# Attention scores by quarters of the array, and h by column halves, in a kernel of chunk attention and two experts

## The chip, the cores and the metric

One core of one Trainium2 chip. The time is that of the device for one execution, in microseconds; the kernel before took 1265.45 us (median of 3 runs).

## The reference

Three stages follow each other; all of them are in float32. B, H, S, D are 8, 8, 576, 64.

```python
q_c, k_c, v_c = (a.reshape(B, H, S // 64, 64, D) for a in (q, k, v))
scores = D ** -0.5 * q_c @ k_c.transpose(0, 1, 2, 4, 3)
attn = np.exp(scores - scores.max(-1, keepdims=True))
attn = attn / (attn.sum(-1, keepdims=True) + 1e-09)
x = (attn @ v_c).reshape(B, H, S, D).transpose(0, 2, 1, 3).reshape(4608, 512)

h = x @ w_in                                  # 512 -> 1024
e = np.exp(h - h.max(-1, keepdims=True))
u = h * (e / (e.sum(-1, keepdims=True) + 1e-09))
mu = u.mean(-1, keepdims=True); var = ((u - mu) ** 2).mean(-1, keepdims=True)
y = ((u - mu) / np.sqrt(var + 1e-06) * g_ln) @ w_out

h2 = y @ w_in2                                # 512 -> 2048
out = np.maximum(0.01 * h2, h2) @ w_out2
```

The weights arrive as 64-bit floats; the kernel converts them itself.

## The kernel before

There are 36 tiles of 128 tokens (`T = 36`). A tile holds two chunks of 64 tokens (index c in the code) for eight heads; two heads (index e) lie one above the other on the 128 partitions, and four such pairs (`KD = 4`) side by side. The order of all instructions is written out by hand (`manual_schedule`): every engine gets its own instructions in the order in which the program calls them.

The first part, up to about 556 us, is one loop over t. In the iteration of t the kernel works on several tiles at once: the scores of tile t + 3 (t + 2 in the first five iterations, `AHEAD = 5`), the softmax of the same, the probabilities' transposition and the product with v for tile t + 1, the first product h of tile t, the activation SoLU and the sums of the layer norm of tile t - 1, the transposition of the normalised tile t - 2, and one group of 24 matmuls of the second product y. Beside that it converts the weights of all products from 64-bit words, in pieces (one or two in an iteration, `DOUBLE`), on ScalarE, VectorE and GpSimd. The second part, the second expert, runs from there to the end; it takes its data through DRAM.

What an iteration calls, in the order of the program, for t > 5 and not "late":

- `solu_a(t-1)`: VectorE's maximum over the 1024 columns of h (L438), ScalarE's exponential with its sum (L440)
- `ff1_mm(t, 0)`: the first 12 matmuls of h of tile t (L423)
- `solu_b(t-1)`: VectorE's product of h and exponential with its sum (L445)
- `pt_mm(t+1)` (L379), `softmax_b(t+2)`: VectorE's sum and reciprocal (L366 to L368), GpSimd's multiplication of es (L369)
- `convert_a`, `convert_b`: VectorE's conversions (L108 to L118); for the pieces of w_out GpSimd's scaling by g (L171)
- `pt_copy(t+1)`: ScalarE's copy of the probabilities (L385)
- `solu_c(t-1)`: GpSimd's small columns (L451, L454, L455), ScalarE's square with its sum (L457), which has the product's sum as its bias; `solu_d(t-1)`: GpSimd normalises (L463 to L467)
- `y1_group`: 24 matmuls of y (L505), ScalarE's copy of y (L513)
- `attend(t)`: x of tile t + 1 (L395), scores of tile t + 3 (L346), the split of x into a high part (ScalarE, L409) and a low part (VectorE, L413), the start of softmax (VectorE L357, L359; ScalarE L362)
- `lnT_mm(t-2)`: eight transposes in two halves (L478), `lnT_split`: high part on ScalarE (L489), low part on VectorE (L493)
- `ff1_mm(t, 1)`: the other 12 matmuls of h

Every fourth iteration (t = 5, 9, 13, ... 33) is "late": the transposes and the split stand ahead of x there, and the group of y stands at the end. In the iterations up to t = 5 the group of y is missing, the conversions stand at the end, and x of the next tile comes after the second half of h. In the code's first stretch (before the loop) `exponentials`, `maxima`, `factors` and `probabilities` do the softmax of tiles 0 to 2.

PSUM has eight banks. Before: two for `ef` (in turn for lnT's halves and for y), four for h (two tiles of two banks), one `ptx` for the probabilities and x, one `s` for the scores. Since `ef` has two banks, the first half of lnT waits for an earlier user, and the second half for the copy of the y of the same iteration.

The scores of a pair of heads come from one matmul for each chunk: q of both heads is stationary (128 rows, 64 columns), and the moving operand is a tile `kbd` in which the keys of the two heads stand on the diagonal, with zeros beside them, so that 128 columns come out.

Of the kernel before, what the change touches and what calls it, by code (L numbers as in the profile page):

```python
# [17 lines left out]
P = 128  # L18
# [3 lines left out]
FF1 = 1024  # L22
# [30 lines left out]
def kernel(  # L53
# [252 lines left out]
    with tc.manual_schedule():  # L306

        with ExitStack() as phase:
# [4 lines left out]
                tc.tile_pool(name="psh", bufs=2, space=bass.MemoryType.PSUM)  # L313
# [4 lines left out]
            kbd = [pa.tile([P, 2, KD, 2, D], F32, tag=f"kbd{i}", bufs=1, name=f"kbd{i}") for i in range(2)]  # L318
# [4 lines left out]
            def load_qk(t, eng=sync):  # L323
# [4 lines left out]
                kb = kbd[t % 2]  # L328
                for e in range(2):
                    eng.dma_start(out=kb[e * D : (e + 1) * D, e], in_=k[t, e * D : (e + 1) * D])  # L330
# [10 lines left out]
            def qk_mm(t):  # L341
                ps = s_ps[t] = bank("ef" if t in (1, 2) else "s", "s_ps").rearrange("p (h n) -> p h n", h=H)
                kb, qq = kbd[t % 2], qt.pop(t)
                for i in range(KD):
                    for c in range(2):
                        pe.matmul(  # L346
                            ps[c * D : (c + 1) * D, 2 * i : 2 * i + 2, :],
                            lhsT=qq[:, i, c * D : (c + 1) * D],
                            rhs=kb[:, :, i, c, :],
                            start=True,  # L350
                            stop=True,
                        )

            def softmax_a(t):
                ps = s_ps.pop(t)
                sm = st8[t] = pa.tile([P, 2, H], F32, tag="st8", name="st8")
                dve.reduce_max(sm[:, 0, :], ps, axis=AX)  # L357
                e = es[t] = pa.tile([P, H, D], F32, tag="es", name="es")
                dve.tensor_tensor(  # L359
                    e, ps, sm[:, 0, :].unsqueeze(2).to_broadcast([P, H, D]), op=ALU.subtract  # L360
                )
# [53 lines left out]
            def ff1_mm(t, half):  # L415
                if half == 0:
                    hs[t] = psh.tile([P, 2, 512], F32, tag="h", name="h_ps")
                x, h = xs[t], hs[t]
                for kk in (0, 1) if half == 0 else (2, 3):
                    w = slots["wi1", kk // 2].rearrange("p e (a n f) -> p e a n f", a=2, n=2)  # L420
                    for a, b in ((0, 0), (0, 1), (1, 0)):
                        for n in range(2):
                            pe.matmul(  # L423
                                h[:, n, :],
# [9 lines left out]

            def solu_a(t):
                h = hs[t].rearrange("p n f -> p (n f)")
                z = sol[t] = wk.tile([P, 8], F32, tag="z", bufs=3, name="z")
                dve.reduce_max(z[:, 0:1], h, axis=AX, negate=True)  # L438
# [164 lines left out]
            def warm(n):  # L603
                for _ in range(n):
                    pe.transpose(spare[:, 0, :P], ident, ident)
# [485 lines left out]
```

## Time and profile before

| what | value |
|---|---|
| median of 3 runs | 1265.45 us (1265.34 to 1266.11) |
| profiled execution, its own time | 1266.24 us |
| span of its instructions | 1264.5 us |
| PE, busy | 1237.8 us, 98% of the span, 7978 instructions |
| DVE, busy | 874.0 us, 69% |
| ACT, busy | 566.5 us, 45% |
| POOL, busy | 269.7 us, 21% |
| mean granted TensorE clock | 0.997 |

PE is TensorE's matmuls, PEld its weight loads, DVE is VectorE, ACT ScalarE, POOL GpSimd. A float32 matmul of the program appears as two instructions of PE. Shares over the span mix the first part with the second, so they say little of an engine's load in one iteration.

### The profile page before, as it was taken

The numbers are of one execution on the slowest core, as the hardware profiler recorded it, in microseconds if no ns is written. First come the engines' busy times: TensorE is split into PE (matmuls) and PEld (weight loads), VectorE is DVE, ScalarE is ACT, GpSimd is POOL, SyncE is SP. The second block draws the span as 40 slices with busy tenths as digits, with TensorE's granted clock in tenths as the row PEclk, the third lists the DMA queues.
The fourth block names the chain that finished last, engine by engine and source line by source line (L and its number), as shares of the span: only waits on it lengthen the run. The fifth ranks groups of instructions, "written<-read, shape, count | busy, mean of one in ns | idle before, by whom it ended". The sixth has DMA issues, their size and how long they took to land.

```text
span 1264.5 us, 21471 instructions
## 1 busy us (share of the span) xinstructions
PE 1237.8 (98%) x7978; PEld 1100.1 (87%) x7978; DVE 874.0 (69%) x1356; ACT 566.5 (45%) x1006; POOL 269.7 (21%) x356
## 2 busy tenths in 40 slices
PE   5999999999999999999999999999999999999998
PEld 4778888878888887899989988998999899989987
DVE  8677767867786777435686677577657766775675
ACT  6646444545544555334433344344235343442351
POOL 0356545644655565200000000000000000000000
PEclk9999999999999999999999999999999999999999
DMA  9525456755575573549889878987898899789676
GB/s 245 155 79 173 147 162 204 237 185 159 187 227 184 162 233 101 192 137 332 265 293 306 294 240 275 309 272 243 293 310 254 260 296 304 242 260 299 202 217 199
DMA packets 171639, 288.74 MB, mean 228 GB/s; under 512 B 50576, under 2 KB 81296, under 8 KB 170512
## 3 DMA queue, kind: packets, MB, share of 16 engines
q1 hardware_dynamic: 171152, 286.78, 71.7%
q8 instruction: 64, 1.05, 0.3%
q10 hardware_dynamic: 384, 0.59, 0.1%
q14 instruction: 39, 0.32, 0.1%
HBM read 239.08 MB, written 48.23 MB: 227 GB/s over the span
## 4 chain that ended last, share of the span: by engine, by line
PE 88%; DVE 6%; ACT 2%; DMA 2%; issue 1%; POOL 0%; SPq 0%; ACTq 0%
PE h_ps L835 28%; PE o_ps L892 19%; PE y_ps L505 14%; PE h_ps L423 12%; PE o_ps L903 10%; PE x_ps L395 2%; PE s_ps L346 2%; PE ln_ps L478 2%; PE pt_ps L379 1%; DVE lnT L493 1%; DVE wf L114 1%; DMA kbd<-in_k 1%; DMA raw<-in_w_in 1%; DVE us L445 1%; DVE wf L110 1%
## 5 line engine op out<-in xcount | busy, mean ns | idle before, releaser
L835 PE MATMUL h_ps<-yo,w_s 128*128 128x384 f32 x2016 | 351.0, 334 | 0.0
L835 PEld LDWEIGHTS h_ps<-yo,w_s 128*128 128x128 f32 x2016 | 349.3, 188 | 0.7
L892 PE MATMUL o_ps<-wo_s,yo 128*128 128x512 f32 (+1 forms) x1016 | 262.9, 393 | 0.0
L423 PE MATMUL h_ps<-wi,xs 128*128 128x512 f32 x864 | 209.9, 396 | 2.8 <-ACT xs L409 1.6
L505 PE MATMUL y_ps<-lnT,wo 128*128 128x512 f32 (+1 forms) x888 | 205.6, 388 | 2.7 <-DVE lnT L493 1.9
L892 PEld LDWEIGHTS o_ps<-wo_s,yo 128*128 128x128 f32 x1016 | 179.0, 188 | 28.7
L505 PEld LDWEIGHTS y_ps<-lnT,wo 128*128 128x128 f32 x888 | 161.0, 188 | 37.4 <-DVE lnT L493 4.4
L423 PEld LDWEIGHTS h_ps<-wi,xs 128*128 128x128 f32 x864 | 159.1, 188 | 37.9 <-ACT xs L409 2.6
L903 PEld LDWEIGHTS o_ps<-wo_s,yo 128*128 128x128 f32 x1008 | 144.6, 188 | 15.6
L271 DVE TENSOR_TENSOR yo<-c,yo 128x768 fp32r<-128x768 f32 x144 | 132.4, 951 | 32.0 <-ACT yo L270 32.0
L903 PE MATMUL o_ps<-wo_s,yo 128*128 128x256 f32 x1008 | 149.7, 283 | 0.0
L814 ACT ACTIVATE c<-h_c 128x384 f32<-128x384 f32 x144 | 72.9, 526 | 127.3 <-DVE h_c L846 127.3
L846 DVE TENSOR_TENSOR h_u<-h_ps,h_p 128x384 f32<-128x384 f32 x96 | 53.2, 554 | 106.8 <-PE h_ps L835 100.0
L270 ACT ACTIVATE yo<-c 128x768 fp32r<-128x768 f32 x144 | 113.0, 835 | 7.1 <-DVE c L876 5.5
L445 DVE SCALAR_TENSOR_TENSOR us<-h_ps,us 128x1024 f32<-128x1024 f32 x36 | 44.1, 1224 | 50.9 <-ACT us L440 50.9
L369 POOL TENSOR_TENSOR es<-es,st 128x512 f32<-128x512 f32 x33 | 34.6, 1047 | 163.7 <-DVE st L368 163.7
L493 DVE TENSOR_TENSOR lnT<-ln_ps,lnT 128x512 fp32r<-128x512 f32 x72 | 46.1, 682 | 33.4 <-ACT lnT L489 33.3
L270 ACT ACTIVATE yo<-a 128x768 fp32r<-128x768 f32 x36 | 29.8, 837 | 72.5 <-DVE a L265 72.5
L846 DVE TENSOR_TENSOR h_c<-h_ps,h_u 128x384 f32<-128x384 f32 x96 | 53.1, 553 | 12.8 <-PE h_ps L835 12.3
L440 ACT ACTIVATE us<-h_ps,z 128x1024 f32<-128x1024 f32 x36 | 40.1, 1115 | 43.0 <-DVE z L438 42.9
L362 ACT ACTIVATE es<-es 128x512 f32<-128x512 f32 x33 | 20.9, 632 | 82.7 <-DVE es L359 82.4
L814 ACT ACTIVATE c<-h_ps 128x384 f32<-128x384 f32 x48 | 23.6, 492 | 76.2 <-PE h_ps L835 76.2
(91 smaller groups left out, 1412.9 us busy)
## 6 DMA issues: line engine op xcount, KB each, us to landing
w_s<-wi_d SPq DMA_DIRECT2D x336, 256.0 KB, 4.0
wo_s<-wo_d SPq DMA_DIRECT2D x168, 512.0 KB, 4.6
wi_d<-wi SPq DMA_DIRECT2D x8, 1792.0 KB, 6.5
wo_d<-wi SPq DMA_DIRECT2D x8, 1792.0 KB, 6.7
raw<-in_w_out SPq DMA_DIRECT2D x24, 512.0 KB, 4.8
raw<-in_w_in SPq DMA_DIRECT2D x23, 512.0 KB, 5.1
vbd<-in_v SPq DMA_DIRECT2D x72, 128.0 KB, 4.3
a<-y_d SPq DMA_DIRECT2D x24, 384.0 KB, 5.2
```

Source lines behind the costliest of these rows:

```text
L270: act.activation(o[:, 0], x, AF.Copy)
L271: dve.tensor_tensor(o[:, 1], x, o[:, 0].bitcast(F32), op=ALU.subtract)
L423: pe.matmul(h[:, n, :], lhsT=x[:, a, kk, :], rhs=w[:, b, kk % 2, n, :], start=(kk == 0 and a == 0 and b == 0), stop=(kk == KD - 1 and a == 1),
L440: act.activation(u, h, AF.Exp, bias=z[:, 0:1], accum_out=z[:, 1:2])
L445: dve.scalar_tensor_tensor(u, h, 1.0 / FF1, u, op0=ALU.mult, op1=ALU.mult, accum_out=z[:, 2:3])
L493: dve.tensor_tensor(dst[:, 1], ps, dst[:, 0].bitcast(F32), op=ALU.subtract)
L505: pe.matmul(ps[:, part], lhsT=w[:, a, kk % 4, m * P : (m + 1) * P], rhs=lnT[:, c, kk, pairs, :][:, part], start=(kk == 0 and a == 0 and c ...
L814: act.activation(blocks[block, j // 2][:, j % 2], src, AF.Prelu, alpha=0.01)
L835: pe.matmul(ps, lhsT=w[:, a, kk * P : (kk + 1) * P], rhs=y[:, c, kk, :], start=(first and kk == 0 and a == 0 and c == 0), stop=(kk == 1 an ...
L846: dve.tensor_tensor(o, ps, x, op=ALU.add)
L892: pe.matmul(ps[:, : 2 * P * (a.stop - a.start)], lhsT=x[:, 0, kk, m * P : (m + 1) * P], rhs=w[:, kk, a].rearrange("p a n -> p (a n)"), sta ...
L903: pe.matmul(sums[p % 2][m][:, : 2 * P], lhsT=x[:, 1, kk, m * P : (m + 1) * P], rhs=w[:, kk, 0], start=False, stop=(i == PAIRS - 1 and kk = ...
```

## The change

- Scores: the key tile has no zeros any more (`kbs`, one DMA). Each head of a pair has its own matmul on 64 rows and 64 columns of the array, so four quarters are in use, and the results of the heads e = 0 and e = 1 go to two banks, `s0` and `s1`. The maxima and the subtraction of the softmax are made bank by bank.
- h: from t = 2 on, the first call of `ff1_mm` computes columns 0 to 511 over all of the contraction, the second columns 512 to 1023. Each half has a bank of its own out of three. The maximum of the first half is taken in the iteration of the tile itself, that of the second in the next; VectorE takes the minimum of the two negated maxima. Exponential and product run by halves, and GpSimd adds the two halves' sums (`solu_c`) ahead of its other columns and of the square.
- In the late iterations the transposes and the split of the layer norm are called ahead of the conversions.
- Names of banks in the second part follow (`s` becomes `s0` or `s1`; one bank of o is now `s1`).

```diff
             psh = phase.enter_context(
-                tc.tile_pool(name="psh", bufs=2, space=bass.MemoryType.PSUM)
+                tc.tile_pool(name="psh", bufs=3, space=bass.MemoryType.PSUM)
...
-            kbd = [pa.tile([P, 2, KD, 2, D], F32, tag=f"kbd{i}", bufs=1, name=f"kbd{i}") for i in range(2)]
+            kbs = [pa.tile([P, KD, 2, D], F32, tag=f"kb{i}", bufs=1, name=f"kb{i}") for i in range(2)]
...
-                kb = kbd[t % 2]
-                for e in range(2):
-                    eng.dma_start(out=kb[e * D : (e + 1) * D, e], in_=k[t, e * D : (e + 1) * D])
+                eng.dma_start(out=kbs[t % 2], in_=k[t])
...
             def qk_mm(t):
-                ps = s_ps[t] = bank("ef" if t in (1, 2) else "s", "s_ps").rearrange("p (h n) -> p h n", h=H)
-                kb, qq = kbd[t % 2], qt.pop(t)
+                ps = s_ps[t] = [
+                    bank("ef" if t == 1 else f"s{e}", "s_ps").rearrange("p (h n) -> p h n", h=H)[:, :KD]
+                    for e in range(2)
+                ]
+                kb, qq = kbs[t % 2], qt.pop(t)
                 for i in range(KD):
-                    for c in range(2):
-                        pe.matmul(
-                            ps[c * D : (c + 1) * D, 2 * i : 2 * i + 2, :],
-                            lhsT=qq[:, i, c * D : (c + 1) * D],
-                            rhs=kb[:, :, i, c, :],
-                            start=True,
-                            stop=True,
-                        )
+                    for e in range(2):
+                        r = slice(e * D, (e + 1) * D)
+                        for c in range(2):
+                            pe.matmul(
+                                ps[e][c * D : (c + 1) * D, i, :],
+                                lhsT=qq[r, i, c * D : (c + 1) * D],
+                                rhs=kb[r, i, c, :],
+                                start=True,
+                                stop=True,
+                            )
...
-                dve.reduce_max(sm[:, 0, :], ps, axis=AX)
                 e = es[t] = pa.tile([P, H, D], F32, tag="es", name="es")
-                dve.tensor_tensor(
-                    e, ps, sm[:, 0, :].unsqueeze(2).to_broadcast([P, H, D]), op=ALU.subtract
-                )
+                for i in range(2):
+                    dve.reduce_max(sm[:, 0, i::2], ps[i], axis=AX)
+                for i in range(2):
+                    m = sm[:, 0, i::2].unsqueeze(2).to_broadcast([P, KD, D])
+                    dve.tensor_tensor(e[:, i::2], ps[i], m, op=ALU.subtract)
...
-                if half == 0:
-                    hs[t] = psh.tile([P, 2, 512], F32, tag="h", name="h_ps")
-                x, h = xs[t], hs[t]
-                for kk in (0, 1) if half == 0 else (2, 3):
+                if t < 2:
+                    ks, ns = ((0, 1), (2, 3))[half], (0, 1)
+                else:
+                    ks, ns = range(KD), (half,)
+                for n in ns if t >= 2 or half == 0 else ():
+                    if t == 1 and n == 1:
+                        hs[t, n] = bank("ef", "h_ps")
+                    else:
+                        hs[t, n] = psh.tile([P, 512], F32, tag="h", name="h_ps")
+                x = xs[t]
+                for kk in ks:
                     w = slots["wi1", kk // 2].rearrange("p e (a n f) -> p e a n f", a=2, n=2)
                     for a, b in ((0, 0), (0, 1), (1, 0)):
-                        for n in range(2):
+                        for n in ns:
                             pe.matmul(
-                                h[:, n, :],
+                                hs[t, n],
                                 lhsT=x[:, a, kk, :],
                                 rhs=w[:, b, kk % 2, n, :],
...
+            def solu_max(t, n):
+                if n == 0:
+                    sol[t] = wk.tile([P, 12], F32, tag="z", bufs=3, name="z")
+                dve.reduce_max(sol[t][:, 8 + n : 9 + n], hs[t, n], axis=AX, negate=True)
+
             def solu_a(t):
-                h = hs[t].rearrange("p n f -> p (n f)")
-                z = sol[t] = wk.tile([P, 8], F32, tag="z", bufs=3, name="z")
-                dve.reduce_max(z[:, 0:1], h, axis=AX, negate=True)
+                z = sol[t]
+                dve.tensor_tensor(z[:, 0:1], z[:, 8:9], z[:, 9:10], op=ALU.min)
                 u = us[t] = wk.tile([P, FF1], F32, tag="us", bufs=3, name="us")
-                act.activation(u, h, AF.Exp, bias=z[:, 0:1], accum_out=z[:, 1:2])
+                for n in range(2):
+                    c = slice(n * 512, (n + 1) * 512)
+                    act.activation(
+                        u[:, c], hs[t, n], AF.Exp, bias=z[:, 0:1], accum_out=z[:, 8 + n : 9 + n]
+                    )
 
             def solu_b(t):
-                h = hs.pop(t).rearrange("p n f -> p (n f)")
                 z, u = sol[t], us[t]
-                dve.scalar_tensor_tensor(
-                    u, h, 1.0 / FF1, u, op0=ALU.mult, op1=ALU.mult, accum_out=z[:, 2:3]
-                )
+                for n in range(2):
+                    c = slice(n * 512, (n + 1) * 512)
+                    dve.scalar_tensor_tensor(
+                        u[:, c],
+                        hs.pop((t, n)),
+                        1.0 / FF1,
+                        u[:, c],
+                        op0=ALU.mult,
+                        op1=ALU.mult,
+                        accum_out=z[:, 10 + n : 11 + n],
+                    )
...
                 z, u = sol[t], us[t]
+                for n in (1, 2):
+                    a = 6 + 2 * n
+                    pool.tensor_tensor(
+                        z[:, n : n + 1], z[:, a : a + 1], z[:, a + 1 : a + 2], op=ALU.add
+                    )
...
-                eng.memset(kbd[i][0:D, 1], 0.0)
-                eng.memset(kbd[i][D:P, 0], 0.0)
...
+                    if t < 3:
+                        solu_max(t - 1, 0)
+                    solu_max(t - 1, 1)
                     solu_a(t - 1)
...
@@ -737,6 +770,10 @@
                     softmax_b(t + 2)
                 if t <= AHEAD or (late and t < T - 1):
                     pt_copy(t + 1)
+                if late and t >= 2:
+                    lnT_mm(t - 2)
+                    lnT_split(t - 2, 0)
+                    lnT_split(t - 2, 1)
                 if t > AHEAD:
                     if late:
                         take_magnitudes(pieces)
@@ -744,10 +781,8 @@
                     convert_b(pieces)
                 if AHEAD < t < T - 1 and not late:
                     pt_copy(t + 1)
-                if late and t >= 2:
-                    lnT_mm(t - 2)
-                    lnT_split(t - 2, 0)
-                    lnT_split(t - 2, 1)
+                if 1 < t < T:
+                    solu_max(t, 0)
                 if 1 <= t <= T:
                     solu_c(t - 1)
                     solu_d(t - 1)
...
```

## Rows read from the trace of the kernel before

**Rows 1.** Stretches: length, then busy us of PE, PEld, DVE, ACT, POOL; granted clock; DMA.
```profile
66.24:503.29 437.05, 429.80 (x3202) 355.03 (x3201) 326.75 (x520) 224.30 (x394) 246.61 (x306) 1.00 0.57 175
...
109.41:123.81 14.40, 14.40 (x110) 11.94 (x109) 11.16 (x19) 8.42 (x15) 9.39 (x13) 1.00 0.58 163
...
555.76:1264.50 708.74, 705.11 (x4040) 659.94 (x4039) 475.67 (x711) 279.96 (x456) 0.00 (x0) 1.00 0.84 271
```

**Rows 2.** Waits of the whole span: engine, line, releaser: us, times, longest.
```profile
PEld x_ps L395 <- ACT pt L385: 7.6, 10, 2.7
...
PEld y_ps L505 <- DVE lnT L493: 4.4, 8, 1.7
```

**Rows 3.** Timeline of TensorE, t = 6: start us, us, engine, line, operation.
```profile
101.03 1.15 PE L395 MATMUL x_ps<-pt,vbd 128*64 128x64 f32 x32
...
102.01 1.05 PE L346 MATMUL s_ps<-kbd,qt 128*64 128x128 f32 x16
...
102.99 0.86 PEld L478 LDWEIGHTS ln_ps<-ident,us 128*128 128x128 f32 x8 [0.17 <-issue]
```

**Rows 4.** Instruction groups by line and shape, VectorE.
```profile
L438 DVE TENSOR_REDUCE z<-h_ps 128x1 f32<-128x1024 f32 x36 | 43.7, 1214 | 3.7 <-PE h_ps L423 3.7
...
L357 DVE TENSOR_REDUCE st<-s_ps 128x8 f32<-128x512 f32 x33 | 22.3, 677 | 0.0
```

**Rows 5.** Timeline of ScalarE and GpSimd, t = 3.
```profile
60.64 1.15 ACT L457 ACTIVATE sq<-us,z 128x1024 bf16<-128x1024 f32 x1
...
61.78 1.06 ACT L489 ACTIVATE lnT<-ln_ps 128x512 fp32r<-128x512 f32 x2
...
62.74 0.59 ACT L409 ACTIVATE xs<-x_ps 128x512 fp32r<-128x512 f32 x1
...
62.95 0.19 POOL L451 TENSOR_SCALAR z<-z 128x1 f32<-128x1 f32 x1
...
63.22 0.19 POOL L454 TENSOR_TENSOR z<-z 128x1 f32<-128x1 f32 x1
```

**Rows 6.** The same, t = 1 (first two) and t = 2.
```profile
43.22 0.60 ACT L409 ACTIVATE xs<-x_ps 128x512 fp32r<-128x512 f32 x1 [0.48 <-PE x_ps L395]
...
43.83 0.19 POOL L451 TENSOR_SCALAR z<-z 128x1 f32<-128x1 f32 x1
...
50.53 0.19 POOL L451 TENSOR_SCALAR z<-z 128x1 f32<-128x1 f32 x1
...
52.20 0.60 ACT L409 ACTIVATE xs<-x_ps 128x512 fp32r<-128x512 f32 x1 [1.77 <-PE x_ps L395]
```

**Rows 7.** Timeline of GpSimd, t = 6, and in the last row t = 7.
```profile
103.08 2.42 POOL L171 TENSOR_TENSOR wf<-wf,g_sb 128x512 f32<-128x512 f32 x2 [2.84 <-DVE wf L118]
...
105.59 0.19 POOL L451 TENSOR_SCALAR z<-z 128x1 f32<-128x1 f32 x1
...
119.23 0.19 POOL L451 TENSOR_SCALAR z<-z 128x1 f32<-128x1 f32 x1
```

**Rows 8.** Stretches at t = 4, columns as in rows 1.
```profile
70.22:73.00 2.78, 0.48 (x8) 0.22 (x8) 2.75 (x6) 2.53 (x5) 0.02 (x1) 1.00 0.85 280
...
73.00:76.40 3.40, 3.40 (x49) 3.07 (x46) 1.61 (x5) 3.01 (x6) 2.07 (x6) 0.50 0.34 99
```

**Rows 9.** Timeline of GpSimd and VectorE, t = 12 (first two) and t = 16.
```profile
188.07 0.65 POOL L454 TENSOR_TENSOR z<-z 128x1 f32<-128x1 f32 x1
...
189.42 0.69 DVE L413 TENSOR_TENSOR xs<-x_ps,xs 128x512 fp32r<-128x512 f32 x1
...
246.90 0.24 POOL L451 TENSOR_SCALAR z<-z 128x1 f32<-128x1 f32 x1
...
247.23 0.65 POOL L454 TENSOR_TENSOR z<-z 128x1 f32<-128x1 f32 x1
...
248.50 0.68 DVE L413 TENSOR_TENSOR xs<-x_ps,xs 128x512 fp32r<-128x512 f32 x1
```

More of the change, by code (lines that the diff above doesn't have):

```diff
@@ L473, in lnT_mm @@
                 for hf in range(2):
-                    tag = ("s", "ptx")[hf] if t == T - 2 else "ef"
+                    tag = ("s0", "ptx")[hf] if t == T - 2 else "ef"
                     ps = ln_ps[t, hf] = bank(tag, "ln_ps").rearrange("p (i n) -> p i n", i=4)
@@ L496, in y1_group @@
                 pairs = (slice(0, 2), slice(0, 3, 2), slice(1, 3))[b % 3]
-                bnk = bank("s" if (b, m) == (NB - 1, 0) else "ef", "y_ps")
+                bnk = bank("s1" if (b, m) == (NB - 1, 0) else "ef", "y_ps")
                 ps = bnk.rearrange("p (a n) -> p a n", a=2)
@@ L577, in exponentials @@
                         es[t][:, h],
-                        ps[:, h],
+                        ps[h % 2][:, h // 2],
                         AF.Exp,
@@ L587, in maxima @@
                 es[t] = pa.tile([P, H, D], F32, tag="es", name="es")
-                dve.reduce_max(sm[:, 0, :], s_ps[t], axis=AX)
+                for i in range(2):
+                    dve.reduce_max(sm[:, 0, i::2], s_ps[t][i], axis=AX)
                 dve.tensor_scalar_mul(sm[:, 0, :], sm[:, 0, :], -scale)
@@ L599, in probabilities @@
                     act.activation(es[t][:, h], es[t][:, h], AF.Copy, scale=sm[:, 1, h : h + 1])
-            spare = psh.tile([P, 2, 512], F32, tag="h", name="spare")
+            spare = psh.tile([P, 512], F32, tag="h", name="spare")
             def warm(n):
                 for _ in range(n):
-                    pe.transpose(spare[:, 0, :P], ident, ident)
+                    pe.transpose(spare[:, :P], ident, ident)
             qk_mm(0)
@@ L825, in h2_product @@
                 if i == 0:
-                    banks[n, chain] = bank(("ptx", "s")[at], "h2_ps")[:, :TH]
+                    banks[n, chain] = bank(("ptx", "s0")[at], "h2_ps")[:, :TH]
                 else:
@@ L916, in out_banks @@
             if p == 1:
-                sums[1] = [pso.tile([P, 512], F32, tag=f"b{m}", name="o_ps") for m in range(3)]
+                sums[1] = [pso.tile([P, 512], F32, tag=f"b{m}", name="o_ps") for m in range(2)]
+                sums[1].append(bank("s1", "o_ps"))
             else:
@@ L921, in out_banks @@
                 if apart:
-                    sums[0][:2] = [bank(tag, "o_ps") for tag in ("ptx", "s")]
+                    sums[0][:2] = [bank(tag, "o_ps") for tag in ("ptx", "s0")]
                 sums["whole"] = None if apart else o
```

## Prediction

> **What bounds the kernel now.** I read the stretches first. From 66 to 503 us, where attention and the first expert run interleaved, TensorE is busy 429.80 of 437.05 us, and in the second expert behind it 705.11 of 708.74 [rows 1]; there the change only gives other bank names. So work taken off TensorE counts, and so does every hole cut into its queue. Then the waits [rows 2]: what holds TensorE is small, 7.6 us of weight loads behind the probabilities' copy (L385) and 4.4 us behind the split of the layer norm (L493). Last the timeline, tile by tile, for who stands behind whom. Two things matter there. In the first tiles (t = 1 to 5 of the loop) TensorE is not the bound: ScalarE, VectorE and GpSimd pass each tile on, and the next h waits for the split of x. From t = 6 on TensorE has no slack, but it needs ScalarE in every tile: the layer norm's second half takes its bank from the copy of y (L513).
>
> **Scores by quarters.** Today a tile's 16 score instructions of 128 columns take 102.99 - 102.01 = 0.98 us, and the 32 of 64 columns before them 102.01 - 101.03 = 0.98 us [rows 3]: the two column halves already overlap, since 0.98/32 = 0.031 us is about half of what 64 columns cost if 128 cost 0.98/16 = 0.061. After: 32 instructions of 64 columns. If all four quarters run at once, half of 0.98, so 0.49; if only the column halves do, 0.98 as in the row above. The layout now changes between x and the scores too; at the change behind the scores the weight load waits 0.17 us for nothing that the profile shows [rows 3]. So a tile gains 0.49 at best, loses 0.17 at worst. I take four at once and one more change: 0.49 - 0.17 = 0.32, call it 0.3. The row is nearest to that, because the column halves overlap fully.
>
> The Trainium skill has a rule against this edit: in TensorEngine Tiling, Key Properties, a change of tiling mode (not of the tile alone) drains the engine. The 0.17 us of rows 3 agrees that a change costs; by that rule the gain is 0.3 a tile, and by a free change it would be 0.49.
>
> **The loads and the masks.** K comes in one DMA in place of two, and the zeroed key tiles go. Both sit ahead of the first scores or beside a busy TensorE: I count nothing, with half a microsecond either way.
>
> **h by halves, on VectorE.** A maximum over 1024 takes 1.214 us, over 512 0.677 [rows 4], so a split costs 2 x 0.677 - 1.214 = 0.14. There are four such splits (maximum of h, product, maximum of scores, subtraction), and a minimum of one column: below 0.8 us a tile. Against it the first half's exponential lets the product start after half of ScalarE's work, and the first half's maximum moves out of the way. I count the two as equal, bounds -0.5 to +0.5 a tile. Where TensorE leads this is hidden.
>
> **The sums of the halves, on GpSimd.** This is the costly edit. The square (L457, ScalarE) takes the product's sum as its bias. VectorE delivers it with the product today. Afterwards GpSimd adds two columns first, and those adds stand where L451 stands now: behind the multiplication of es (L369), which waits for softmax's reciprocal. At t = 3 the square starts at 60.64, L451 only at 62.95 [rows 5]. L451 with the gap behind it takes 0.27 there and L454, an addition of one column, 0.19; from these I take 0.45 for two adds. So the square starts at 62.95 + 0.45 = 63.40, 2.8 us late, and what is behind it on ScalarE moves too: 63.40 + 1.14 for the square (61.78 - 60.64) + 0.96 for the two lnT copies (62.74 - 61.78) = 65.50 for the copy of x, which started at 62.74. That is +2.8 on the path, since h of the next tile needs x.
>
> - t = 4 has the same pattern: +2.8.
> - t = 1: 43.83 + 0.45 + 1.14 = 45.42 for x, not 43.22: +2.2 [rows 6].
> - t = 2: 50.53 + 0.45 + 1.14 + 0.96 = 53.08, not 52.20: +0.9 [rows 6].
> - t = 5 is late by little; not counted.
>
> First tiles: 2.8 + 2.8 + 2.2 + 0.9 = +8.7 us. The three banks of h also make the second half of h wait for the first half of the tile before (the product at t = 3); but that ends before the late copy of x and is covered by it. If TensorE were at half clock there the cover would fail, which is the upper bound of +13; the lower is 6, with VectorE's gain taken at every tile.
>
> At t = 6 and 7 GpSimd has two scalings of w_out (L171) ahead of L451, which wait for VectorE's conversions. At t = 6 the sum is ready at 105.59 + 0.45 = 106.04, the square ends its turn at 107.18, and the copy of y, as long as that of x (0.60 [rows 6]), ends at 107.78 [rows 7]. TensorE wants that bank for the second half of lnT, four transposes after 102.99, at 103.43. It stands for 4.3 us, and the copy of x behind it is late by as much, so VectorE's conversions and L171 of t = 7 are too. There L451 comes at 119.23 today [rows 7]; 4.3 us later and with the adds, square and copy it is 119.23 + 4.3 + 0.45 + 1.14 + 0.60 = 125.7, where the second half of lnT is due one tile (14.40 us [rows 1]) after 103.43, at 117.8: +7.9. With the two tiles' 0.3 us on TensorE taken off, t = 6 and 7 together: +7.3 (bounds 5.5 and 9).
>
> A stand of that length also lowers the clock: after 70.22 to 73.00, in which TensorE worked 0.48 of 2.78 us, it was granted half, 1.2 GHz, for 3.40 us [rows 8]. One such stretch costs 3.40/2 = 1.7. That behind t = 6 falls into the wait of t = 7; that behind t = 7 counts: +1.7 (0 to 3.4).
>
> **From t = 9 on** the loop repeats every eight tiles, three times. At t = 16 L451 comes at 246.90, and beside VectorE an add costs 0.65 (L454) [rows 9]: sum at 246.90 + 1.2 = 248.1, square to 249.25, copies of y and x start at 249.25 and 249.75, x's low part at 250.4 in place of 248.50, +1.9; VectorE carries it through the next tile's exponential to the probabilities' copy, which TensorE waits for in the late tiles (L385 in rows 2). I take +1.7. At t = 12 L454 runs at 188.07, and by the same steps the low part of x, 189.42 today, comes near 190.5 [rows 9]; an estimate is that half of it is slack, +0.6. The split ahead of the conversions takes away what is left of the wait of L505 in the late tiles, -0.6 (4.4 us over 8 waits [rows 2]), and four of the eight tiles keep their 0.3: -1.2. Sum +0.5 for eight tiles, +1.5 for 24. Bounds -4.5 (0.49 a tile, t = 12 without a wait) to +6 (quarters that don't overlap).
>
> **Sum.** 8.7 + 7.3 + 1.7 + 1.5 = +19.2 us. The profiled execution took 1266.24 us with a span of 1264.5; the median of the runs is 1265.45, 0.8 below it. 1266.24 + 19.2 = 1285.4 for such an execution, and 1284.7 for the median; I say 1285.
>
> **Rivals.**
> - *The square stays hidden, faster.* If the sum reaches ScalarE within the idle time ahead of its next work, all waits fall away; then some 33 tiles give 0.3 us, 9.9, and three late tiles 0.6, 1.8: 1253.7. For it: a busy TensorE covers ScalarE in most tiles. It decides at 1.8 us, the longest such idle time in the first tiles [rows 6]; against it, L451 starts 2.3 us behind the square in rows 5. Chance 0.10.
> - *The quarters don't overlap across the row halves.* The edit then does not do what it says: 0.98 + 0.17 for the scores, 0.48 us worse than counted in the some 16 tiles where TensorE sets the pace: +7.7, 1292.4. For it: the trace shows column halves only. Chance 0.13.
> - *TensorE does not wait at t = 6 and 7*, because the two banks of lnT and y fall otherwise. Then 7.3 + 1.7 go: 1275.7. Against it: the bank order follows the calls, and they don't change. Chance 0.10.
> - *About no change*, the losses of the first tiles being half and the gain 0.49: chance 0.04.
>
> My forecast has 0.63. A difference under 0.2% (2.5 us) can hardly be told from none. Slower: 0.63 + 0.13 + 0.10 = 0.86; faster 0.10; same 0.04. The bounds of the terms add to 6 + 5.5 + 0 - 4.5 = +7 and 13 + 9 + 3.4 + 6 = +31; from 1268 to 1298 all slower cases are in and 0.14 is left out.
>
> **What the profile after would show.** Right: the square waits for GpSimd's column in nearly every tile, 2 to 3 us in the first ones and over 7 at t = 6 and 7; TensorE idles some 4 us ahead of the second half of lnT in both of these; 32 score instructions in about half a microsecond. The second expert takes as long as before. Wrong: the square right behind the product, or TensorE without a hole near 105 us. What would undo the prediction most is a first-tile path that has slack that I took for none.

## The result, and the profile after

The changed kernel takes 1279.53 us (median of 5 runs, 1277.58 to 1280.57) against 1265.45: ratio 1.0109, 95% interval 1.0094 to 1.0123, so it is slower by 14 us. The forecast was 1285 with a range of 1268 to 1298. The profiled execution took 1279.53 us with a span of 1277.7, against 1266.24 and 1264.5: 13.3 us more, and the text below accounts for those.

Stretches of the kernel after, columns as in [rows 1]. The first answers to the first of [rows 1], from the transposes of the probabilities at t = 4 to the same point behind the last tiles; the second is the second expert.

```profile
71.68:516.71 445.03, 426.51 (x3666) 350.79 (x3664) 340.47 (x698) 229.05 (x455) 261.12 (x364) 0.99 0.54 171
568.81:1277.70 708.89, 705.05 (x4040) 659.87 (x4039) 475.91 (x711) 279.96 (x456) 0.00 (x0) 1.00 0.85 271
```

The second expert is as long as before (708.89 and 708.74). In the first stretch TensorE has less work (426.51 us for 429.80) and stands idle for 18.5 us, where it was idle for 7.3. So TensorE was indeed relieved, and holes cost more than that was worth. Waits of the whole span, columns as in [rows 2]:

```profile
ACT sq L488 <- POOL z L479: 80.5, 35, 7.0
...
PE ln_ps L509 <- ACT ys L544: 10.5, 5, 3.9
PE h_ps L434 <- ACT xs L413: 5.5, 5, 2.3
PE h_ps L434 <- DVE us L465: 5.5, 2, 2.9
...
PEld x_ps L399 <- ACT pt L389: 5.2, 12, 0.6
```

The square (L488) waits for GpSimd's added column 35 times in 36. Three waits of TensorE hang on it or on the third bank: the layer norm's second half (L509), h for the copy of x, and h for the product that reads its bank (L465). Against that, the wait for the probabilities' copy is shorter than in [rows 2], and that of y for the layer norm's split (4.4 us there) is gone.

Timeline of ScalarE and GpSimd at t = 3, which answers to [rows 5], and ahead of it ScalarE's copies of x at t = 1 and 2, which answer to [rows 6]:

```profile
44.86 0.58 ACT L413 ACTIVATE xs<-x_ps 128x512 fp32r<-128x512 f32 x1
...
54.79 0.60 ACT L413 ACTIVATE xs<-x_ps 128x512 fp32r<-128x512 f32 x1
...
62.59 0.59 ACT L389 ACTIVATE pt<-pt_ps 128x512 f32<-128x512 f32 x1
64.44 1.04 POOL L373 TENSOR_TENSOR es<-es,st 128x512 f32<-128x512 f32 x1 [3.77 <-DVE st L372]
65.45 0.34 POOL L479 TENSOR_TENSOR z<-z 128x1 f32<-128x1 f32 x2
65.82 1.15 ACT L488 ACTIVATE sq<-us,z 128x1024 bf16<-128x1024 f32 x1 [2.64 <-POOL z L479]
66.97 1.06 ACT L520 ACTIVATE lnT<-ln_ps 128x512 fp32r<-128x512 f32 x2
67.92 0.60 ACT L413 ACTIVATE xs<-x_ps 128x512 fp32r<-128x512 f32 x1
```

The square used to follow the copy of the probabilities at once. Now ScalarE stands for 2.64 us, until GpSimd has multiplied es (L373) and made its two additions (0.34 us, together with the gap behind them 0.4). The copy of x starts 1.6, 2.6 and 5.2 us later than in [rows 5, 6].

GpSimd and ScalarE at t = 6 and 7, which answer to [rows 7], and TensorE at t = 6, which answers to [rows 3]:

```profile
109.04 2.42 POOL L171 TENSOR_TENSOR wf<-wf,g_sb 128x512 f32<-128x512 f32 x2 [2.84 <-DVE wf L118]
111.42 0.33 POOL L479 TENSOR_TENSOR z<-z 128x1 f32<-128x1 f32 x2
...
111.79 1.15 ACT L488 ACTIVATE sq<-us,z 128x1024 bf16<-128x1024 f32 x1 [6.97 <-POOL z L479]
112.94 0.58 ACT L544 ACTIVATE ys<-y_ps 128x512 f32<-128x512 f32 x1
...
130.51 0.33 POOL L479 TENSOR_TENSOR z<-z 128x1 f32<-128x1 f32 x2
```

```profile
107.25 1.15 PE L399 MATMUL x_ps<-pt,vbd 128*64 128x64 f32 x32
108.34 0.69 PE L349 MATMUL s_ps<-kb,qt 64*64 64x64 f32 x32
108.96 0.66 PE L509 MATMUL ln_ps<-ident,us 128*128 128x128 f32 x4
113.57 1.11 PE L509 MATMUL ln_ps<-ident,us 128*128 128x128 f32 x4 [3.95 <-ACT ys L544]
...
132.66 1.11 PE L509 MATMUL ln_ps<-ident,us 128*128 128x128 f32 x4 [2.20 <-ACT ys L544]
```

This is the chain of the forecast, link by link: scalings, additions, square, copy of y, and TensorE's second four transposes 3.95 us late at t = 6 and 2.20 us at t = 7. The scores now take 108.96 - 108.34 = 0.62 us instead of 0.98, and the product with V before them 1.09 instead of 0.98.

Stretches at the stand of t = 6, behind it and behind that of t = 7, and then two at t = 4, which answer to [rows 8]:

```profile
109.70:113.57 3.87, 0.00 (x1) 0.01 (x1) 0.47 (x1) 1.78 (x4) 2.94 (x9) 0.82 0.80 261
112.20:119.00 6.80, 5.43 (x15) 4.47 (x16) 3.30 (x7) 4.44 (x9) 3.08 (x6) 0.50 0.73 228
132.70:136.10 3.40, 3.40 (x10) 2.85 (x11) 2.02 (x5) 1.32 (x3) 1.71 (x2) 0.50 0.80 258
70.30:76.05 5.75, 2.85 (x20) 2.31 (x18) 5.61 (x14) 1.96 (x6) 1.47 (x2) 1.00 0.28 86
76.05:79.45 3.40, 3.40 (x26) 2.63 (x28) 2.10 (x6) 0.76 (x3) 1.53 (x4) 1.00 0.48 167
```

TensorE was granted half (1.2 GHz) for 6.8 us behind t = 6 and for 3.4 us behind t = 7. In early_from_8 (below), whose program is the same up to t = 7, it was 3.4 us behind t = 6 and none behind t = 7, so these lengths differ from run to run. At t = 4, where [rows 8] show 0.50, the clock stays full: there it had worked 2.85 us of the 5.75 before, in place of 0.48 of 2.78.

Instruction groups of VectorE and GpSimd by shape, which answer to [rows 4]:

```profile
L449 DVE TENSOR_REDUCE z<-h_ps 128x1 f32<-128x512 f32 x72 | 48.8, 680 | 4.0 <-PE h_ps L434 3.9
...
L479 POOL TENSOR_TENSOR z<-z 128x1 f32<-128x1 f32 x72 | 18.1, 272 | 10.7 <-ACT us L457 9.6 <-DVE us L465 1.1
```

A maximum over half a row takes 680 ns (677 expected), an addition on GpSimd 272 ns in the mean.

To see where the time arises, the following table takes one start in each tile, that of ScalarE's copy of x, and subtracts its start in the kernel before. It is worked out from the traces of the profiled executions; the columns are the pass t of the loop, the rows the kernels that are told below.

```
late, us      t=0   t=1   t=2   t=3   t=4   t=5    t=6    t=7    t=8   t=18   t=26   t=34
after       -0.47 +1.63 +2.58 +5.18 +6.40 +6.32 +11.16 +15.85 +16.40 +14.92 +14.25 +13.42
relay       -0.32 +1.66 +2.30 +4.85 +6.03 +6.22 +11.34 +15.31 +14.31 +16.32 +18.26 +20.15
early_67    -0.54 +1.58 +3.09 +6.00 +7.38 +7.30  +7.17  +6.91  +6.64  +5.18  +4.30  +3.60
early_from_8 -0.76 +1.33 +2.91 +5.84 +7.22 +7.15 +11.99 +15.47 +14.45 +12.11 +11.08 +9.53
adds_early  -0.84 -0.99 -0.09 +2.98 +2.92 +2.74  +2.64  +2.37  +2.11  -0.25  -1.60  -3.42
early_swap  -0.77 -0.92 -0.01 +0.31 +0.34 +1.19  +1.09  +0.82  +0.55  -1.86  -3.19  -5.32
early_halves -0.50 -0.49 +0.44 +2.01 +3.75 +3.55 +3.45  +3.44  +3.42  +2.67  +3.05  +1.53
lnt_only    +1.07 -0.35 -0.36 -0.35 -0.36 -1.15  -1.19  -1.20  -1.19  -2.11  -2.20  -3.79
```

For the changed kernel: -0.5 us in the start, +6.8 from t = 0 to 5, +10.1 from t = 5 to 8, -3.0 from there to t = 34, and -0.1 in the rest.

### The profile page after: what moved, and what is told of

It is laid out like the page before. It is cut to its first block, busy times and chain, and to the rows that moved or that the text cites. A ratio compares the mean times of both kernels' runs of the same rounds, so it can differ in the third digit from the quotient of the medians.

```text
span 1277.7 us, 22962 instructions
## 1 busy us (share of the span) xinstructions
PE 1234.1 (97%) x8554; PEld 1094.5 (86%) x8554; DVE 891.3 (70%) x1567; ACT 572.9 (45%) x1078; POOL 287.5 (22%) x426
## 4 chain that ended last, share of the span: by engine, by line
PE 80%; DVE 10%; ACT 4%; DMA 2%; issue 2%; POOL 2%; SPq 0%; POOLq 0%; ACTq 0%
PE h_ps L870 27%; PE o_ps L927 18%; PE y_ps L536 11%; PE o_ps L938 9%; PE h_ps L434 9%; PE x_ps L399 2%; DVE us L465 1%; PE ln_ps L509 1%; DMA kb<-in_k 1%; DVE lnT L524 1%; DVE wf L114 1%; DVE wf L108 1%; POOL es L373 1%; DVE wc L191 1%; DVE st L362 1%
## 5 line engine op out<-in xcount | busy, mean ns | idle before, releaser
L434 PE MATMUL h_ps<-wi,xs 128*128 128x512 f32 x864 | 214.8, 401 | 12.3 <-ACT xs L413 5.5
L434 PEld LDWEIGHTS h_ps<-wi,xs 128*128 128x128 f32 x864 | 161.7, 192 | 49.3 <-DVE us L465 6.3
L488 ACT ACTIVATE sq<-us,z 128x1024 bf16<-128x1024 f32 x36 | 41.4, 1150 | 80.5 <-POOL z L479 80.5
L465 DVE SCALAR_TENSOR_TENSOR us<-h_ps,us 128x512 f32<-128x512 f32 x72 | 48.6, 690 | 35.0 <-ACT us L457 35.0
L373 POOL TENSOR_TENSOR es<-es,st 128x512 f32<-128x512 f32 x33 | 34.6, 1048 | 157.3 <-DVE st L372 148.0
L457 ACT ACTIVATE us<-h_ps,z 128x512 f32<-128x512 f32 x72 | 48.7, 682 | 39.1 <-DVE z L453 39.1
L417 DVE TENSOR_TENSOR xs<-x_ps,xs 128x512 fp32r<-128x512 f32 x36 | 24.7, 687 | 51.4 <-ACT xs L413 51.4
```

Of the source, the lines that this page charges most:

```text
L434: pe.matmul(hs[t, n], lhsT=x[:, a, kk, :], rhs=w[:, b, kk % 2, n, :], start=(kk == 0 and a == 0 and b == 0), stop=(kk == KD - 1 and a == 1),)
L457: act.activation(u[:, c], hs[t, n], AF.Exp, bias=z[:, 0:1], accum_out=z[:, 8 + n : 9 + n])
L465: dve.scalar_tensor_tensor(u[:, c], hs.pop((t, n)), 1.0 / FF1, u[:, c], op0=ALU.mult, op1=ALU.mult, accum_out=z[:, 10 + n : 11 + n],)
```

## The experiments

Theory 1 was the forecast's: the square, late by GpSimd's queue, makes the loss. Its main rival was that h's third bank does, in the first tiles at least. Each kernel is timed against the kernel before on the same chip. That kernel took 1265.45 to 1266.23 us there, so differences of up to 0.8 us between two kernels can come from the chips. The medians less that of the kernel before beside them:

```
after +14.1   relay +20.7   early_67 +3.8     early_from_8 +10.7   dve_sum +4.2      adds_early -1.2   early_swap -3.3
col_halves +15.1   early_halves +3.2   lnt_only -2.9   lnt_behind +17.7   copy_late -3.7   copy_first -4.8
```

**relay.** The wait alone, put into the kernel before:

```diff
-  act.activation(u, h, AF.Exp, bias=z[:, 0:1], accum_out=z[:, 1:2])
+  act.activation(u, h, AF.Exp, bias=z[:, 0:1], accum_out=z[:, 8:9])
   (the product's accum_out likewise: z[:, 10:11] for z[:, 2:3])
 def solu_c(t):
+  for n in (1, 2):
+      pool.tensor_tensor(z[:, n:n+1], z[:, 6+2*n:7+2*n], zero, op=ALU.add)
```

> The kernel before, with nothing of the change but that both sums pass through an addition of zero on GpSimd at the head of solu_c, where the change has its two additions. h stays whole in its two double banks, the scores stay by column halves. Theory 1 (the wait alone makes the loss): the square late by 2 to 3 us at t = 1 to 4 and by about 7 at t = 6 and 7; +7 and +10 us, +1 for later tiles where nothing is gained on TensorE: 1283.5 us (1280 to 1287). Theory 2 (three banks of h and the order of its halves carry part of the loss): 1270 to 1278.

Measured 1286.44 us, ratio 1.0162 (1.0147 to 1.0177): theory 1, at the top of its range. Waits of this kernel:

```profile
ACT sq L463 <- POOL z L454: 91.4, 34, 7.5
...
PE ln_ps L484 <- ACT ys L519: 9.3, 5, 4.0
```

The row of relay in the table follows that of the changed kernel to within 0.4 us up to t = 6. So the late square is enough to make the loss of the first tiles and of t = 6 and 7. From t = 5 to 8 it makes +8.1 us where the changed kernel has +10.1; here the half-clock stretch behind t = 6 is 3.4 us and not 6.8, and behind t = 7 there is none. From t = 8 on, where this kernel gains nothing, it loses 5.8 us more.

**early_67.** GpSimd's additions queued right behind the product, at t = 6 and 7 alone:

```diff
   solu_b(t - 1)
+  if t in (6, 7):
+      solu_sums(t - 1)   # the two additions; at other t they stay in solu_c
```

> The changed kernel with GpSimd's additions queued right behind the product at t = 6 and 7 alone; everywhere else they stand where the change put them. Theory 1 (the late sum at t = 6 and 7 costs what the prediction said, by the copy of y and a half clock behind the stand): the step from t = 5 to t = 9 falls from +10.4 us to about 0, 1269.5 us (1267.5 to 1271.5). Theory 2 (another stand shows in its place, as GpSimd's scaling of w_out holds the layer norm too): 1274 to 1278.

Measured 1269.98 us, ratio 1.0029 (1.0018 to 1.0040): theory 1. From t = 5 to 8 this kernel moves by -0.7 us in the table instead of +10.1, and TensorE runs the eight transposes of t = 6 in one go:

```profile
109.28 0.69 PE L349 MATMUL s_ps<-kb,qt 64*64 64x64 f32 x32
109.91 1.09 PE L514 MATMUL ln_ps<-ident,us 128*128 128x128 f32 x8
110.76 5.74 PE L434 MATMUL h_ps<-wi,xs 128*128 128x512 f32 x24
```

**early_from_8.** The same from t = 8 on, and not before:

```diff
+  if t > 7:
+      solu_sums(t - 1)
```

> The changed kernel with the additions queued early from t = 8 on, and where the change put them before that. Theory 1 (the late square costs some 2 us in eight tiles from t = 9 on, as the relay through GpSimd alone showed, +1.95 us in eight): 6 us less, 1273.5 us (1272 to 1275.5). Theory 2 (the late tiles take the wait up with slack of their own): 1 us less, 1278.5 (1277 to 1280).

Measured 1276.9 us, ratio 1.0087 (1.0071 to 1.0102): 2.6 us less than the changed kernel, or 3.4 us with each set against the kernel before beside it: between the theories. In the traces this kernel gains 4.9 us from t = 8 to 34, where the changed kernel gains 3.0. TensorE at t = 16 and 17, first in the changed kernel, then in this one:

```profile
261.81 0.66 PE L509 MATMUL ln_ps<-ident,us 128*128 128x128 f32 x4
263.94 0.66 PE L509 MATMUL ln_ps<-ident,us 128*128 128x128 f32 x4 [1.48 <-ACT ys L544]
...
271.71 1.15 PE L399 MATMUL x_ps<-pt,vbd 128*64 128x64 f32 x32 [0.31 <-ACT pt L389]
```

```profile
259.21 1.09 PE L514 MATMUL ln_ps<-ident,us 128*128 128x128 f32 x8
...
268.87 1.15 PE L399 MATMUL x_ps<-pt,vbd 128*64 128x64 f32 x32 [1.76 <-ACT pt L389]
```

The stand of 1.48 us at t = 16 is gone, and in the late tile behind it TensorE waits 1.76 us for the probabilities' copy, where it waited 0.31. So at this place nothing is gained: 1.48 + 0.31 against 1.76.

**dve_sum** and **adds_early.** Two ways to take the square's wait away everywhere:

```diff
 def solu_b(t):               # dve_sum
+  dve.tensor_tensor(z[:, 2:3], z[:, 10:11], z[:, 11:12], op=ALU.add)
 def solu_b(t):               # adds_early: both additions from solu_c to here
+  for n in (1, 2):
+      pool.tensor_tensor(z[:, n:n+1], z[:, 6+2*n:7+2*n], z[:, 7+2*n:8+2*n], op=ALU.add)
```

> The changed kernel, but VectorE itself adds the two columns of the product's sum, right behind the product; GpSimd keeps the addition for the exponentials' sum. Theory 1 (the square's wait for GpSimd sets the loss): the waits of the square go, with them the +7 us of t = 1 to 4, the +10 us of t = 6 and 7, the stands of TensorE ahead of the second half of lnT, and the quarters' gain of some 0.25 us a tile stays: 1261.5 us (1259 to 1264). Theory 2 (in the first tiles the wait of h's second half for its third bank costs the time, the square only at t = 6 and 7): 1269 (1267 to 1272). Theory 3 (the square's wait goes but what it hid, VectorE's longer chain, comes out instead): 1275 or more.

> The changed kernel with both additions still on GpSimd, but queued right behind the product, ahead of the multiplication of es and ahead of the scalings of w_out. Theory 1 (the place in GpSimd's queue is what costs): within 2 us of the kernel in which VectorE adds, 1262.5 us, with the square starting about 0.5 us behind the product. Theory 2 (the crossing to GpSimd and back costs, wherever it stands): 1272 to 1280. Also possible: the multiplication of es comes later by the two additions, 0.4 us, which the next pt_mm would show as some 0.4 us a first tile, 1264.

Measured 1269.91 us for dve_sum, ratio 1.0033 (1.0020 to 1.0045), the time of theory 2; and 1264.49 us for adds_early, ratio 0.9990 (0.9981 to 0.9999), theory 1 of that run by its own time, 2 us above it, but not within 2 us of dve_sum. The square's wait falls from 80.5 us to 5.0 in adds_early, though the additions stay on GpSimd: it was their place in the queue that cost. Yet the first tiles still lose 3.9 us from t = 1 to 4 (table), at t = 2 and 3; so the time of 1264 us that was named as possible came by another wait than the one named there. TensorE at t = 3 and 4 of adds_early, and then of dve_sum:

```profile
60.01 4.21 PE L434 MATMUL h_ps<-wi,xs 128*128 128x512 f32 x12 [2.61 <-DVE us L465]
...
73.61 3.06 PE L434 MATMUL h_ps<-wi,xs 128*128 128x512 f32 x12 [2.64 <-DVE us L465]
```

```profile
61.69 4.38 PE L434 MATMUL h_ps<-wi,xs 128*128 128x512 f32 x12 [2.63 <-DVE us L465]
...
75.31 4.34 PE L434 MATMUL h_ps<-wi,xs 128*128 128x512 f32 x12 [2.66 <-DVE us L465]
```

The second half of h stands 2.6 us for its bank, until the product of the tile before has read it, and the next tile's product with V stands in the queue behind. Twelve matmuls that take 3.06 us at full clock take 4.2 to 4.4 where a half-clock stretch falls on them: one of these in adds_early, two in dve_sum. At t = 8 dve_sum is 3.7 us behind adds_early, which is about two more stretches (it has one more at t = 1), and from there to t = 34 it gains 2.5 us where adds_early gains 5.5: its TensorE waits for the probabilities' copy 8.2 us in 9 waits, not 5.2 in 3. How much of the 5.4 us between the medians is chance of the clock stays open.

**early_swap.** adds_early, with the next tile's attention ahead of that second half at t = 3 and 4:

```diff
+  if t in (3, 4):
+      attend(t)        # and not behind it, as at the other t up to 5
   if t < T:
       ff1_mm(t, 1)
```

> The kernel with GpSimd's additions queued early, and at t = 3 and 4 attention's next tile (its product with V, the split of x) is issued ahead of the second half of h, so that it no longer stands behind that half's wait for its bank. Theory 1 (without the square's wait the bank wait of three-bank h holds the first tiles: TensorE stands 2.6 us at t = 3 and at t = 4 and the next x is late by 3 us): the first tiles end some 3 us earlier, 1261 us (1258.5 to 1263). Theory 2 (the first tiles are held by VectorE's longer chain, not by the bank): no change, 1264.5.

Measured 1262.74 us, ratio 0.9972 (0.9961 to 0.9982): theory 1, by the trace too: t = 1 to 4 lose 1.3 us and not 3.9. At t = 5 this kernel loses 0.9 us where adds_early gains 0.2, so that 1.6 of the 2.6 us are left, near the 1.8 us between the medians and less than the 3 us expected. It is faster than the kernel before and the changed one. What TensorE waits for at t = 3 and 4 is now the probabilities:

```profile
60.63 1.30 PE L399 MATMUL x_ps<-pt,vbd 128*64 128x64 f32 x32 [3.18 <-ACT pt L389]
...
72.83 1.15 PE L399 MATMUL x_ps<-pt,vbd 128*64 128x64 f32 x32 [1.66 <-ACT pt L389]
```

**col_halves** and **early_halves.** The scores by column halves again, in the changed kernel and in adds_early:

```diff
-  for e in range(2):
-      pe.matmul(ps[e][c*D:(c+1)*D, i, :], lhsT=qq[r, i, c*D:(c+1)*D], rhs=kb[r, i, c, :])
+  pe.matmul(ps[c*D:(c+1)*D, 2*i:2*i+2, :], lhsT=qq[:, i, c*D:(c+1)*D], rhs=kb[:, :, i, c, :])
```

> The changed kernel with the scores as before, by column halves over the full height of the array with the zeroed key tiles, one bank a tile, two banks in turn. Theory 1 (the four quarters overlap and TensorE sets the pace from t = 9): 0.25 us more in each of some 25 tiles, +6: 1285.5 us (1283 to 1288). Theory 2 (the scores' time is hidden by the waits): 1279.5, no difference.

> The kernel with GpSimd's additions queued early, and with the scores by column halves as before. It prices the quarters where no square waits. Theory 1 (0.26 us a tile on TensorE wherever TensorE sets the pace): 0.26 x 27 = 7 us more than with the quarters, 1271.5 us (1269.5 to 1273.5). Theory 2 (half of the tiles hide it behind other waits, as in the changed kernel): 1267.5 (1266 to 1269).

Measured 1280.79 us, ratio 1.0121 (1.0105 to 1.0136), near theory 2, and 1269.26 us, ratio 1.0029 (1.0020 to 1.0039), between the theories. By the medians the quarters are worth 1.3 us with the late square, which is not clear of the noise, and 4.8 without it. But that the late square hides them the traces do not show: from t = 8 to 34 the quarters give 3.3 us with it (-3.0 in the changed kernel, +0.3 in col_halves) and 3.6 without it (-5.5 in adds_early, -1.9 in early_halves), some 0.13 us a tile, though the single tile that TensorE paces falls by 0.26. What differs lies ahead of that: at t = 8 col_halves is 2.5 us less late than the changed kernel, and its half-clock stretch behind t = 6 is 3.4 us long with none behind t = 7, as in early_from_8.

**lnt_only** and **lnt_behind.** The third part alone, and the change without it:

```diff
   pt_copy(t + 1)
+  if late and t >= 2:        # lnt_only; lnt_behind moves the same lines back
+      lnT_mm(t - 2); lnT_split(t - 2, 0); lnT_split(t - 2, 1)
   ...convert_a, convert_b
```

> The kernel before with the third part of the change alone: in the late tiles (one in four) the layer norm's transposes and split stand ahead of the conversions. Theory 1 (most of what the tiles from t = 9 on gained beyond the quarters is this): 0.5 to 1 us for each of 8 late tiles, 1259.5 us (1257 to 1262). Theory 2 (it takes away 0.4 us a wait at most, as the waits of y for lnT add to 4.4 us over 8, and the copy of the probabilities waits longer instead): 1264 (1262.5 to 1265.5).

> The changed kernel with the third part undone: in the late tiles the layer norm's transposes and split stand behind the conversions again, as before. Theory 1 (the order is worth 0.5 to 1 us a late tile also beside the later square): 1285 us (1283 to 1288). Theory 2 (it is worth little): 1280.5 (1279 to 1282).

Measured 1263.18 us, ratio 0.9975 (0.9966 to 0.9984), theory 2; and 1283.76 us, ratio 1.0142 (1.0128 to 1.0156): 4.2 us more than the changed kernel, inside theory 1's range, and 2.9 us of them arise from t = 8 to 34.

**copy_late** and **copy_first.** An attempt at more: early_swap, with the copy of the probabilities ahead of h's exponentials in the late tiles, and in copy_first at t = 3 and 4 too:

```diff
+  if late and AHEAD < t < T - 1:     # copy_first: or t in (3, 4)
+      ff1_mm(t, 0); pt_mm(t + 1); pt_copy(t + 1)
   solu_a(t - 1)
```

> The kernel with early additions and the swap at t = 3 and 4, and in the late tiles past t = 5 the copy of the transposed probabilities stands ahead of the exponentials of h in ScalarE's queue, since the transposes are done before the exponentials may start. Theory 1 (TensorE's wait for that copy, 1.74 us at t = 17 and its like, three times, and shorter ones, goes): 1257.5 us (1256 to 1260). Theory 2 (the exponentials come later by the copy and the wait returns at the square or at x): 1262.

> The same, and at t = 3 and 4 too the copy of the probabilities stands ahead of the exponentials. Theory 1 (there the next tile's product with V waited 3.2 and 1.7 us for that copy, and x follows it): 2 to 4 us less than with the late tiles alone, 1254.5 us. Theory 2 (the copy of x stands behind the square and the layer norm's copies on ScalarE anyway): within 1 us of the kernel with the late tiles alone.

Measured 1262.5 us, ratio 0.9971 (0.9959 to 0.9982), and 1261.42 us, ratio 0.9958 (0.9945 to 0.9970). copy_late has the time of theory 2, but by a wait that neither theory named; copy_first is 1.1 us below it, close to theory 2 and far from theory 1. TensorE at t = 17 of copy_late:

```profile
254.82 1.15 PE L399 MATMUL x_ps<-pt,vbd 128*64 128x64 f32 x32
257.42 0.69 PE L349 MATMUL s_ps<-kb,qt 64*64 64x64 f32 x32 [1.45 <-DMA kb<-in_k]
```

The wait of 1.74 us is gone, and the scores right behind wait 1.45 us for the load of K. From t = 5 to 34 copy_late gains 6.7 us and early_swap 6.5. copy_first has the lowest median of all, but its interval overlaps that of early_swap.

## Why the prediction came out right, point by point

**Scores by quarters**, +0.3 us a tile: right. Per tile 0.98 + 0.98 became 1.09 + 0.62, so 0.25 us less. The quarters overlap across the row halves: 32 instructions of 64 columns take 0.98 us as column halves (the product with V) and 0.62 us as quarters, with a change of layout in it. That makes four at a time only if the column halves overlap too, and the prediction's reason for that does not hold: 0.031 us for 64 columns and 0.061 for 128 are the same price per column. The gain does not hang on it. The rival without overlap (1292.4) falls. The layout change costs 0.11 us more ahead of the scores, for early_halves, which keeps the column halves beside all the rest, has 0.98 there (from 104.48 to 105.46 us). The Trainium skill, TensorEngine Tiling (Array Packing), Key Properties, says that a change of mode drains the engine; by that rule some loss per tile was due, and the 0.11 us agree.

**Loads and masks**, nothing: 0.5 us gained by t = 0, at the bound given.

**h by halves, on VectorE**, nothing: not settled alone. 680 ns for a half confirms the row it was taken from. From t = 8 the splits and the third part together gave 1.9 us (early_halves), and the third part alone 2.6 (lnt_only), so the splits cost 0.7 us there, if the two add, which no run shows.

**First tiles**, +8.7 us, measured +6.8. Per tile, t = 1: +2.1 (forecast 2.2), t = 2: +0.95 (0.9), t = 3: +2.6 (2.8), t = 4: +1.2 (2.8). Only t = 4 is off, though the square waits there as it does at t = 3, for 2.64 us. The difference is made by VectorE, between the copies of x of t = 3 and 4. Its two conversions ahead of h's maximum and GpSimd beside them, first in the kernel before, then in the changed one:

```profile
65.17 1.09 DVE L108 TENSOR_SCALAR wf<-wf 128x512 f32<-128x512 f32 x1
65.94 1.45 POOL L125 TENSOR_TENSOR wo<-wf,wo 128x512 fp32r<-128x512 f32 x1
66.29 1.38 DVE L110 TENSOR_SCALAR wf<-wf 128x512 uint32<-128x512 uint32 x1
```

```profile
69.43 1.30 POOL L125 TENSOR_TENSOR wo<-wf,wo 128x512 fp32r<-128x512 f32 x1
70.35 0.66 DVE L108 TENSOR_SCALAR wf<-wf 128x512 f32<-128x512 f32 x1
71.05 0.43 DVE L110 TENSOR_SCALAR wf<-wf 128x512 uint32<-128x512 uint32 x1
```

They take 1.09 us instead of 2.47, so 1.4 us of the 2.6 come back. In the kernel before GpSimd's L125 ran beside both, in the changed one it was done soon after the first had begun; that this is what made them short is argued from these rows and was not tried. In relay, whose t = 4 adds 1.2 us too, the two take 0.67 and 0.43 us. The half-clock stretch of [rows 8], which is gone too, is not the cause: in lnt_only there is none either, and its t = 4 is as early as its t = 3 (-0.36 and -0.35). The forecast carried the lateness on with VectorE's times unchanged.

**The bank wait, covered**: right for the changed kernel, since the copy of x was later still, but it is a second cause and not a free one. With the square on time the first tiles still lose 3.9 us (adds_early). Once the attention no longer stands behind the bank wait (early_swap), 2.6 of these come back by t = 4, and past t = 5 1.6 are left. Late square and late bank run side by side, so removing the one does not give back its price.

**t = 6 and 7 with the clock**, 7.3 + 1.7 = +9.0, measured +10.1 in the trace, and 9.5 us between the medians of the changed kernel and early_67. The stands are 3.95 and 2.20 us. The forecast had 4.3 us and, with 1.7 us of half clock falling into the second wait, 3.6 - 1.7 = 1.9. The half-clock stretch behind t = 6 was 6.8 us and not 3.4. Part of the good fit is luck: in early_from_8, with the same program up to t = 7 but one stretch of 3.4 us, the stands are 3.98 and 2.23 us and the move is +7.3, which is the term without the clock, and 2.8 us of the +10.1 come and go with the stretches. The rival in which TensorE does not wait there falls.

**From t = 9 on**, +1.5 us, measured -3.0: this is the step that failed in size. Its gains were right: 3.6 us for the quarters and 1.8 for the third part were counted, and adds_early against early_halves shows 3.6 and early_halves, for the third part with the splits, 1.9. Its wait was not: "VectorE carries it through the next tile's exponential to the probabilities' copy, which TensorE waits for", +1.7, with t = 12 +2.3 in eight tiles and 6.9 in all. Between the changed kernel and adds_early it is worth 2.5, and 2.6 to 3.4 between the medians of the changed kernel and early_from_8. The path was another too: TensorE stands for 1.48 us at t = 16, ahead of the layer norm's second half, and in the late tile behind it waits less for the probabilities' copy, 0.31 us where it waits 1.76 without the stand; only what goes beyond that counts. Over the eight tiles from t = 18 to 26 TensorE's idle time is nearly the same in both, 2.27 us of 116.15 in the changed kernel and 2.13 of 115.48 in adds_early, so by which waits the 2.5 us arise stays open. In the kernel before, a somewhat longer wait of the square (up to 3.0 us, where the changed kernel has 2.5) does cost 5.8 (relay).

The terms that missed, -0.5 at the start, -1.9, +1.1, -4.5 and -0.1 behind t = 34, add to -5.9; with them the forecast of +19.2 becomes +13.3, the difference of the spans. So the two waits that make the loss were foreseen, and the time came out 6 us lower mainly because the wait from t = 9 on was priced too high.

The rival that the square stays hidden (1253.7) falls twice: it waits 35 times, and with it on time the kernel takes 1264.49, as the bank wait is left and a tile keeps less than 0.3 us.

That quarters would need two banks, and h three, was not tried in another way. The Trainium skill, TensorEngine Tiling (Array Packing), Gotcha 1, says that different row tiles cannot use one bank at the same time. No run here shows it.

## What to carry to other kernels

A tiny instruction that is moved to an in-order engine costs what stands ahead of it in that queue: two additions, 0.34 us together, made the square wait up to 7.0 us, and queued earlier they left 5.0 of 80.5 us of its waits. Price a wait against the next wait on the same path, since a stand ahead of one that was due anyway costs little, and two waits that run side by side are not given back by removing one. When engines shift against each other, their times may change too: two conversions on VectorE took 2.47 us in one kernel and 1.09 in the other. And before the clock is made the cause of a difference, look for a run in which the stretch is missing and the difference is not.

## What the runs showed of the hardware

The length of the half-clock stretches was not expected: 3.4 us behind most stands, but 6.8 us behind that of t = 6 in the changed kernel, where TensorE worked 0.00 of the 3.87 us before. In relay, after a stand of 4.00 us at the same place, it was one of 3.4 us, and so it was in early_from_8 after 3.98 us, though its program is the same as the changed kernel's up to there. Their number varies too: in the first 82 us past the start-up there was none in lnt_only, one in adds_early and three in dve_sum.
